# A transformer block's first microseconds: one input tile held back, and its neighbours reordered around the attention weights

## The chip, the cores and the metric

The kernel runs on one core of a Trainium2 chip. The metric is device time in microseconds (us) from start to end of one execution; before the change it is 512.29 us, the median of three runs (512.12 to 512.51). The core has a matrix engine (TensorE, "PE" in the profile, with its weight loads as "PEld"), a vector engine (VectorE, "DVE"), a scalar engine (ScalarE, "ACT"), GpSimd ("POOL") and a synchronising engine (SyncE, "SP") that here mostly starts transfers. Transfers between device memory and on-chip memory run on the core's 16 DMA engines; they are started from a queue of SyncE ("SPq") or of ScalarE ("ACTq").

## The reference

For 2,048 tokens of width 576 the block normalises the input, and adds linear attention with 32 heads and a gated feed-forward part (4,608 wide) to it:

```
xn  = layernorm(x)                                   # 2048 x 576
q, k, v = split(xn @ wqkv)                           # 32 heads of 18
phi = lambda t: where(t > 0, t + 1, exp(t)) + 1e-6
kv  = sum_s phi(k)[s] outer v[s];  z = sum_s phi(k)[s]
o   = (phi(q) @ kv) / (phi(q) . z + 1e-6)
out = x + o @ wo + (gelu(xn @ w_gate) * (xn @ w_up)) @ w_down
```

## The kernel before

**Tiling.** The tokens are handled as 16 tiles of 128 (`NS`), each tile lying on the 128 partitions. One tile of x is 128 rows of 576 bf16, 144 KB. The weights `wqkv` are held as three blocks, Q (0), K (1) and V (2); `load_w` (L107, L108) brings one block in two transfers, 576 KB for rows 0 to 511 and 72 KB for the rest. The V part isn't multiplied tile by tile: a matrix G, the sum over tokens of xn times phi(k), is collected instead (L294), and V's weights come in later.

**Stages.** The first stage goes over the 16 tiles: statistics (L212, two halves, then L215), the reciprocal deviation on ScalarE (`rstd`, L219 and L220), the normalisation (L233 on VectorE; for odd tiles from 3 on, L228 on ScalarE), a transposition to `xnT`, the projections K and Q (L263, ten matmuls of 128x288 each), exp (L270) and phi (L275), and G. Tiles 0 and 1 are transposed by TensorE into PSUM (L248) and copied out (L252), the later ones by DMA. Then G is finished and multiplied with V's weights, and the feed-forward part follows: four chunks of 512 tokens, each with gate and up products (L325) and the down products (L688), in which TensorE reads weights that were loaded some blocks ahead.

**The head.** At the top, SyncE starts tile 0, K's weights, tiles 2 and 3 in one transfer, Q's weights, and tiles 4 to 7, in that order; ScalarE starts tile 1, and then loads the table of its functions (L112). VectorE clears a part of the weights' tile (L118) and fills three constants. TensorE meanwhile multiplies an identity matrix with itself, `NWARM` = 38 times (`spin`, L132), work whose result is never read and which keeps the engine active until the first real work arrives. `spin(2)` comes once more between tile 0's transposes and K's first matmul.

**What sets the order.** From there the order of the instructions on every engine comes from a small planner in the kernel (`in_order`). Each step has an engine, an assumed duration, a rank (its due time in tiles), the steps that it follows, and for those that need a transfer the assumed time of arrival: `X_AT` for tiles of x, `W_AT` for K's and Q's weights. The planner goes through time, and on the engine that is free first takes the step of lowest rank that may start. A tile's `lead` shifts the ranks of its statistics and normalisation. These numbers only set the order; on the chip each instruction waits for what it needs. An engine works its instructions in the order written, so one that waits holds up those behind it.

Of the kernel before, what the change touches and what calls it, by code (L numbers as in the profile page):

```python
# [35 lines left out]
GUB = 2  # L36
NWBUF = 4
WDS = 3
NWARM = 38
TD = 2  # L40
XW = 640
KLO = HP + 1
# [15 lines left out]
def kernel(  # L58
# [11 lines left out]
    nc = tc.nc  # L70
# [19 lines left out]
    x_sb = persist.tile([P, NS, D], BF16, name="x_sb")  # L90

    def load_x(n0, cnt, on=nc.sync):
        on.dma_start(x_sb[:, n0:n0 + cnt, :], x_view[:, n0:n0 + cnt, :])  # L93
# [11 lines left out]
    def load_w(which):  # L105
        c = slice(which * D, (which + 1) * D)
        nc.sync.dma_start(wqkv_sb[:, 0:4, c], A_wqkv[0:512, c].rearrange("(kt p) c -> p kt c", p=P))  # L107
        nc.sync.dma_start(wqkv_sb[0:HP, 4, c], A_wqkv[512:576, c])  # L108

    load_x(0, 1)  # L110
    load_x(1, 1, nc.scalar)
    nc.scalar.preload_act_table_set("natural_log_exp_and_others")  # L112
    load_w(1)
    load_x(2, 2)
    load_w(0)
    load_x(4, 4)

    nc.vector.memset(wqkv_sb[HP:P, 4, :], 0.0)  # L118

    ident = const.tile([P, P], BF16, name="ident")  # L120
    make_identity(nc, ident[:])
# [7 lines left out]
    def spin(count):  # L129

        for _ in range(count):
            nc.tensor.matmul(ps_all[:, 7, 0:P], lhsT=ident[:], rhs=ident[:], start=True, stop=True)  # L132

    spin(NWARM)

# [61 lines left out]
    def z_add(n):  # L197
        nc.gpsimd.tensor_tensor(  # L198
            out=z_bf[:] if n == NS - 1 else z_sum[:], in0=pk[:, 0, 1:D + 1] if n == 1 else z_sum[:], in1=pk[:, n, 1:D + 1],
            op=ALU.add,  # L200
        )
# [7 lines left out]
    def ln_half(n, h):  # L209
        if h == 0:  # L210
            ln_raw[n] = asmall.tile([P, 2, nc.vector.BN_STATS_DIM], F32, name="stats")
        nc.vector.bn_stats(out=ln_raw[n][:, h, :], in_=x_sb[:, n, h * HALF:(h + 1) * HALF])  # L212

    def ln_aggr(n):
        nc.vector.bn_aggr(out=mv[:, n, :], in_=ln_raw[n][:])  # L215

    def ln_rstd(n):
        r = rstd[:, n:n + 1]
        nc.scalar.activation(out=r, in_=mv[:, n, 1:2], func=ACT.Ln, bias=eps_ln[:], scale=1.0)  # L219
        nc.scalar.activation(out=r, in_=r, func=ACT.Exp, scale=-0.5)  # L220

    def ln_bias(n):
        nc.gpsimd.tensor_scalar(
            out=nbias[:, n:n + 1], in0=mv[:, n, 0:1], scalar1=rstd[:, n:n + 1], scalar2=-1.0, op0=ALU.mult, op1=ALU.mult,
        )

    def ln_norm_act(n):
        nc.scalar.activation(  # L228
            out=xn[:, n, 0:D], in_=x_sb[:, n, :], func=ACT.Identity, bias=nbias[:, n:n + 1], scale=rstd[:, n:n + 1],
        )  # L230

    def ln_norm(n, c0=0, c1=D):
        nc.vector.tensor_scalar(  # L233
            out=xn[:, n, c0:c1], in0=x_sb[:, n, c0:c1], scalar1=mv[:, n, 0:1], scalar2=rstd[:, n:n + 1],
            op0=ALU.subtract, op1=ALU.mult,
        )
# [8 lines left out]
    def transposes(n, k0=0, k1=KT, b=None):  # L245
        b = TP_BANK[n] if b is None else b
        for kt in range(k0, k1):
            nc.tensor.transpose(tp_bank(b)[:, kt, :], xn[:, n, kt * P:(kt + 1) * P], ident[:])  # L248

    def tp_copy(n, k0=0, k1=KT, b=None, copy=acopy):  # L250
        b = TP_BANK[n] if b is None else b
        copy(out=xnT[:, k0:k1, n * P:(n + 1) * P], in_=tp_bank(b)[:, k0:k1, :])  # L252

    def dma_transposes(n):
        nc.sync.dma_start_transpose(xnT[:, :, n * P:(n + 1) * P], xn[:, n, 0:640])
# [4 lines left out]
    def kq_mm(n, which, hf):  # L260
        c = which * D + hf * HALF
        for kt in range(KT):
            nc.tensor.matmul(  # L263
                ps_all[:, KQ_BANK[which] + hf, :HALF], lhsT=xnT[:, kt, n * P:(n + 1) * P],
                rhs=wqkv_sb[:, kt, c:c + HALF], start=(kt == 0), stop=(kt == KT - 1),
            )

    def kq_exp(n, which, hf):
        e = e_tiles[n, which, hf] = awork.tile([P, HALF], F32, name="phi_e", tag="phi_e", bufs=8)
        nc.scalar.activation(  # L270
            out=e[:], in_=ps_all[:, KQ_BANK[which] + hf, :HALF], func=ACT.Exp, bias=neg1[:], scale=1.0,
        )

    def kq_phi(n, which, hf):
        nc.vector.scalar_tensor_tensor(  # L275
            out=(pq, pk)[which][:, n, which + hf * HALF:which + (hf + 1) * HALF], in0=e_tiles[n, which, hf][:], scalar=1.0,
            in1=ps_all[:, KQ_BANK[which] + hf, :HALF], op0=ALU.min, op1=ALU.max,
        )
# [12 lines left out]
    def g_accumulate(n, pieces):  # L291
        for kt, ps_ in pieces.items():
            for b, col, d0, w in ps_:
                nc.tensor.matmul(  # L294
                    ps_all[:, b, col:col + w], lhsT=xn[:, n, kt * P:(kt + 1) * P], rhs=pk[:, n, 1 + d0:1 + d0 + w],
                    start=(n == 0 and col == 0), stop=(n == NS - 1), skip_group_check=True,
                )
# [134 lines left out]
    def step(name, *args, **kw):  # L432
        steps[name] = _Step(*args, **kw)

    X_AT = [3.65, 4.20, 6.40, 6.40] + [9.50] * 4
    W_AT = {1: 5.50, 0: 7.60}

    for n0 in range(8, NS, 2):
        step(("x", n0), "SP", 0.50, n0 - 5.5, [], lambda n0=n0: load_x(n0, 2), ready=1.6 * n0 + 2.0, tail=3.0)
    for n in range(NS):  # L440
        lead = {0: -9.0, 1: 0.5, 2: -0.5, 3: -0.5}.get(n, 0.0)
        after_x = [("x", n // 2 * 2)] if n >= 8 else []
        x_at = X_AT[n] if n < 8 else 0.0
        for h in range(2):
            step(("stats", n, h), "DVE", 0.41, n - 2.2 + lead, after_x, lambda n=n, h=h: ln_half(n, h), ready=x_at)
        step(("aggr", n), "DVE", 0.21, n - 2.1 + lead, [("stats", n, 0), ("stats", n, 1)], lambda n=n: ln_aggr(n))
        step(("rstd", n), "ACT", 0.49, n - 2.1 + lead, [("aggr", n)], lambda n=n: ln_rstd(n))
        if n < TD:
            for i, (k0, k1, eng) in enumerate([(0, 3, "ACT"), (3, KT, "ACT" if n else "DVE")]):
                b = TP_BANK[n] - i  # L450
                step(("norm", n, i), "DVE", 0.25, n - 2.1 + lead, [("rstd", n)],
                     lambda n=n, k0=k0, k1=k1: ln_norm(n, k0 * P, min(k1 * P, D)))
                step(("tp", n, i), "PE", 0.20, n - 1.5 + lead, [("norm", n, i)],
                     lambda n=n, k0=k0, k1=k1, b=b: transposes(n, k0, k1, b))
                step(("xnT", n, i), eng, 0.30 if i else 0.48, n - 0.88 + lead, [("tp", n, i)],
                     lambda n=n, k0=k0, k1=k1, b=b, eng=eng: tp_copy(n, k0, k1, b, acopy if eng == "ACT" else vcopy))
            ready = [("xnT", n, 0), ("xnT", n, 1)]
        else:
            if n % 2:
                step(("bias", n), "POOL", 0.15, n - 2.1, [("rstd", n)], lambda n=n: ln_bias(n))  # L460
                step(("norm", n), "ACT", 0.65, n - 2.1, [("bias", n)], lambda n=n: ln_norm_act(n))
            else:
                step(("norm", n), "DVE", 0.43, n - 2.1, [("rstd", n)], lambda n=n: ln_norm(n))
            step(("xnT", n), "SP", 2.10, n - 1.9, [("norm", n)], lambda n=n: dma_transposes(n), tail=1.7)
            ready = [("xnT", n)]
        for which, rank in ((1, n), (0, n + 0.6)):
            for h in range(2):
                r = rank + h / 100
                free = [("phi", n - 1, which, h)] if n else []
                step(("mm", n, which, h), "PE", 0.615, r, ready + free, lambda n=n, w=which, h=h: kq_mm(n, w, h),  # L470
                     ready=W_AT[which], tail=0.15)
                step(("exp", n, which, h), "ACT", 0.49, r + 0.10, [("mm", n, which, h)],
                     lambda n=n, w=which, h=h: kq_exp(n, w, h))
                step(("phi", n, which, h), "DVE", 0.44, r + 0.15, [("exp", n, which, h)],
                     lambda n=n, w=which, h=h: kq_phi(n, w, h))
        if n > 0:
            idle = [("norm", n + 4) if n % 2 == 0 else ("bias", n + 4)] if n + 4 < NS else []
            step(("z", n), "POOL", 1.40, n + 2.0, [("phi", m, 1, h) for m in (0, n) for h in range(2)] + idle,
                 lambda n=n: z_add(n))
        step(("G", n), "PE", 0.75, n + 1.15, [("phi", n, 1, 0), ("phi", n, 1, 1)], lambda n=n: g_accumulate(n, G_A))  # L480
    step(("spin",), "PE", 0.11, -1.0, [("tp", 0, 1)], lambda: spin(2))

    def in_order(steps):

# [281 lines left out]
```

## Time and profile before

| what | us |
|---|---|
| time, median of 3 runs | 512.29 |
| span of the profiled run | 510.7 |
| TensorE busy | 505.2 |
| VectorE busy | 211.4 |
| ScalarE busy | 136.9 |
| tile 0 of x, issue to landing | 3.0 |
| tile 1 of x, issue to landing | 2.9 |
| first statistics start | 3.86 |
| K's first matmul starts | 6.91 |
| Q's first matmul starts | 8.80 |

Times within a run count from the span's start. Busy time of an engine is the time in which one of its instructions is in progress. An arrow in a list of waits names what ended a wait; "idle before" is the idle time of the engine ahead of an instruction. The granted clock of TensorE is 1.000 of full speed over the run.

### The profile page before, as it was taken

The numbers are of one execution on the slowest core, as the hardware profiler recorded it, in microseconds if no ns is written. First come the engines' busy times: TensorE is split into PE (matmuls) and PEld (weight loads), VectorE is DVE, ScalarE is ACT, GpSimd is POOL, SyncE is SP. The second block draws the span as 40 slices with busy tenths as digits, with TensorE's granted clock in tenths as the row PEclk, the third lists the DMA queues.
The fourth block names the chain that finished last, engine by engine and source line by source line (L and its number), as shares of the span: only waits on it lengthen the run. The fifth ranks groups of instructions, "written<-read, shape, count | busy, mean of one in ns | idle before, by whom it ended". The sixth has DMA issues, their size and how long they took to land.

```text
span 510.7 us, 10656 instructions
## 1 busy us (share of the span) xinstructions
PE 505.2 (99%) x4489; PEld 304.6 (60%) x4489; DVE 211.4 (41%) x447; ACT 136.9 (27%) x267; POOL 25.5 (5%) x40
## 2 busy tenths in 40 slices
PE   7999999999999999999999999999999999999997
PEld 6888854444587744444677644444777444445774
DVE  7887455555400045565200254555100356544101
ACT  5887533332310022332100023323000133232000
POOL 3344200000000000000000000000000000000000
PEclk9999999999999999999999999999999999999999
DMA  6633839999500057666300256566100565540000
GB/s 210 144 67 55 244 97 273 279 276 272 147 13 12 1 170 172 154 167 165 87 12 13 69 168 173 156 174 154 35 12 1 144 166 159 164 130 14 13 12 24
DMA packets 119002, 61.26 MB, mean 120 GB/s; under 512 B 25698, under 2 KB 118122, under 8 KB 118954
## 3 DMA queue, kind: packets, MB, share of 16 engines
q1 hardware_dynamic: 118810, 60.43, 45.0%
q8 instruction: 35, 0.57, 0.5%
q10 hardware_dynamic: 144, 0.15, 0.2%
q14 instruction: 13, 0.11, 0.1%
HBM read 52.86 MB, written 2.36 MB: 108 GB/s over the span
## 4 chain that ended last, share of the span: by engine, by line
PE 98%; DMA 1%; SPq 0%; issue 0%; DVE 0%
PE ps_all L325 55%; PE ps_all L688 28%; PE ps_all L263 7%; PE ps_all L294 3%; PE ps_all L693 3%; DMA wqkv_sb<-in_A_wqkv_dram 1%; PE ps_all L676 0%; PE ps_all L301 0%; PE ps_all L374 0%; PE ps_all L628 0%; SPq L93 0%; SPq L108 0%; SPq L107 0%; DVE res L702 0%; PE ps_all L362 0%
## 5 line engine op out<-in xcount | busy, mean ns | idle before, releaser
L325 PE MATMUL ps_all<-xnT,wg 64*128 64x512 bf16 x1152 | 272.1, 376 | 0.0
L325 PE MATMUL ps_all<-xnT,wu 64*128 64x512 bf16 x1152 | 271.6, 376 | 0.0
L617 ACT ACTIVATE gl<-ps_all 128x512 f32<-128x512 f32 x144 | 86.0, 597 | 308.9 <-PE ps_all L325 308.8
L618 DVE TENSOR_TENSOR hT<-ps_all,gl 128x512 bf16<-128x512 f32 x144 | 99.6, 692 | 130.9 <-ACT gl L617 130.4
L325 PEld LDWEIGHTS <-wu 64*128 64x128 bf16 x1152 | 108.4, 94 | 68.1
L325 PEld LDWEIGHTS <-wg 64*128 64x128 bf16 x1152 | 108.4, 94 | 67.7
L688 PE MATMUL ps_all<-wd_sb,hT 128*128 128x288 bf16 (+2 forms) x1152 | 147.1, 286 | 0.0
L688 PEld LDWEIGHTS <-hT 128*128 128x128 bf16 x1152 | 110.8, 98 | 30.9 <-issue 1.2
L702 DVE TENSOR_TENSOR res<-ps_all,x_sb 128x288 bf16<-128x288 f32 (+2 forms) x32 | 13.8, 455 | 146.3 <-PE ps_all L693 88.1
L325 PE MATMUL ps_all<-xnT,wr 64*128 64x512 bf16 x288 | 54.7, 376 | 0.0
L263 PE MATMUL ps_all<-wqkv_sb,xnT 128*128 128x288 bf16 x320 | 42.1, 286 | 0.6 <-DMA wqkv_sb<-in_A_wqkv_dram 0.3
L263 PEld LDWEIGHTS <-xnT 128*128 128x128 bf16 x320 | 30.5, 98 | 7.9 <-ACT xnT L252 0.5
L270 ACT ACTIVATE phi_e<-ps_all,neg 128x288 f32<-128x288 f32 x64 | 30.9, 495 | 9.1 <-PE ps_all L263 6.3
L325 PEld LDWEIGHTS <-wr 64*128 64x128 bf16 x288 | 14.0, 94 | 16.7
L693 PE MATMUL ps_all<-m_sb,pqT 128*128 128x288 bf16 (+2 forms) x128 | 20.9, 286 | 0.0
L294 PE MATMUL ps_all<-hT,xn 128*128 128x288 bf16 (+4 forms) x144 | 18.8, 274 | 0.0
L275 DVE SCALAR_TENSOR_TENSOR pq<-phi_e,ps_all 128x288 bf16<-128x288 f32 x32 | 14.2, 450 | 7.7 <-ACT phi_e L270 7.4
L198 POOL TENSOR_TENSOR z_sum<-z_sum,hT 128x576 f32<-128x576 f32 x13 | 16.2, 1244 | 4.7 <-DVE hT L275 4.4
L294 PEld LDWEIGHTS <-xn 128*128 128x128 bf16 x144 | 14.0, 98 | 3.6 <-issue 0.2
L275 DVE SCALAR_TENSOR_TENSOR hT<-phi_e,ps_all 128x288 bf16<-128x288 f32 x32 | 14.1, 454 | 2.4 <-ACT phi_e L270 2.3
L693 PEld LDWEIGHTS <-pqT 128*128 128x128 bf16 x128 | 12.4, 98 | 3.3
L212 DVE BATCH_NORM_STATS2 stats<-x_sb 128x6 f32<-128x288 bf16 x32 | 13.6, 440 | 1.9 <-DMA x_sb<-in_A_x_dram 1.9
(66 smaller groups left out, 125.3 us busy)
## 6 DMA issues: line engine op xcount, KB each, us to landing
wg<-in_B_w_gate_dram SPq DMA_DIRECT2D x72, 256.0 KB, 3.0
wu<-in_B_w_up_dram SPq DMA_DIRECT2D x72, 256.0 KB, 3.6
wd_sb<-in_B_w_down_dram SPq DMA_DIRECT2D x12, 432.0 KB, 5.4
wr<-in_B_w_gate_dram SPq DMA_DIRECT2D x72, 32.0 KB, 2.8
wr<-in_B_w_up_dram SPq DMA_DIRECT2D x72, 32.0 KB, 3.1
out_dram<-res SPq DMA_DIRECT2D x15, 144.0 KB, 1.8
wqkv_sb<-in_A_wqkv_dram SPq DMA_DIRECT2D x3, 576.0 KB, 4.6
x_sb<-in_A_x_dram SPq DMA_DIRECT2D x5, 288.0 KB, 3.1
```

Source lines behind the costliest of these rows:

```text
L198: nc.gpsimd.tensor_tensor(out=z_bf[:] if n == NS - 1 else z_sum[:], in0=pk[:, 0, 1:D + 1] if n == 1 else z_sum[:], in1=pk[:, n, 1:D + 1], ...
L212: nc.vector.bn_stats(out=ln_raw[n][:, h, :], in_=x_sb[:, n, h * HALF:(h + 1) * HALF])
L263: nc.tensor.matmul(ps_all[:, KQ_BANK[which] + hf, :HALF], lhsT=xnT[:, kt, n * P:(n + 1) * P], rhs=wqkv_sb[:, kt, c:c + HALF], start=(kt == ...
L270: nc.scalar.activation(out=e[:], in_=ps_all[:, KQ_BANK[which] + hf, :HALF], func=ACT.Exp, bias=neg1[:], scale=1.0,)
L275: nc.vector.scalar_tensor_tensor(out=(pq, pk)[which][:, n, which + hf * HALF:which + (hf + 1) * HALF], in0=e_tiles[n, which, hf][:], scala ...
L294: nc.tensor.matmul(ps_all[:, b, col:col + w], lhsT=xn[:, n, kt * P:(kt + 1) * P], rhs=pk[:, n, 1 + d0:1 + d0 + w], start=(n == 0 and col = ...
L325: return nc.tensor.matmul(self.outs[i], lhsT=self.lhs(i, rows, kt), rhs=self.rhs(i, rows, kt), start=start, stop=stop, skip_group_check=True,)
L617: nc.scalar.activation(out=gl[:], in_=ps_all[:, b[0], :], func=ACT.Gelu_apprx_tanh)
L618: nc.vector.tensor_tensor(out=hT[:, GUB * k + i, :], in0=ps_all[:, b[1], :], in1=gl[:], op=ALU.mult)
L688: nc.tensor.matmul(self.acc(hf), lhsT=hT[:, f, j * P:(j + 1) * P], rhs=wd_sb[:, f, self.parts[hf]], start=(f == 0 and not paired), stop=Fa ...
L693: nc.tensor.matmul(self.acc(hf), lhsT=pqT[:, c, self.ts], rhs=m_sb[:, c, self.parts[hf]], start=False, stop=(paired and c == 3), skip_grou ...
L702: nc.vector.tensor_tensor(out=self.res[:, hs], in0=self.acc(hf), in1=x_sb[:, self.n, hs], op=ALU.add)
```

## The change

The change rearranges the transfers at the top and tells the planner. Tile 1's load moves behind a write of one column of its own destination by VectorE (`memset(x_sb[:, 1, 0:1])`); as both write the same place, the load has to wait for it, and with this it starts after tile 0's load instead of together with it. Tiles 2 and 3 are loaded one by one: tile 2 ahead of Q's weights, tile 3 behind them. The planner gets other times of arrival: tile 0 at 3.05 instead of 3.65, tile 2 sooner, tile 3 and tiles 4 to 7 later, Q's weights later. The number of spins before the first transposes falls from 38 to 32, and that of the spins after them rises from 2 to 5. The purpose is to have the first tile there sooner, to have Q's weights not stand behind a tile that isn't needed yet, and to order the head's instructions by what arrives when.

```diff
-NWARM = 38
+NWARM = 32
...
     load_x(0, 1)
-    load_x(1, 1, nc.scalar)
     nc.scalar.preload_act_table_set("natural_log_exp_and_others")
     load_w(1)
-    load_x(2, 2)
+    load_x(2, 1)
     load_w(0)
+    load_x(3, 1)
     load_x(4, 4)
 
     nc.vector.memset(wqkv_sb[HP:P, 4, :], 0.0)
+    nc.vector.memset(x_sb[:, 1, 0:1], 0.0)
+    load_x(1, 1, nc.scalar)
...
-    X_AT = [3.65, 4.20, 6.40, 6.40] + [9.50] * 4
-    W_AT = {1: 5.50, 0: 7.60}
+    LEAD = (-9.0, 0.5, -0.5, -0.5)
+    X_AT = [3.05, 4.30, 6.00, 8.60] + [10.40] * 4
+    W_AT = {1: 5.60, 0: 8.10}
...
-        lead = {0: -9.0, 1: 0.5, 2: -0.5, 3: -0.5}.get(n, 0.0)
+        lead = LEAD[n] if n < 4 else 0.0
...
-    step(("spin",), "PE", 0.11, -1.0, [("tp", 0, 1)], lambda: spin(2))
+    step(("spin",), "PE", 0.30, -1.0, [("tp", 0, 1)], lambda: spin(5))
```

In the instruction lists of the two kernels VectorE has one instruction more, TensorE three matmuls less, and the rest is the same in number but for the one transfer that became two. On TensorE all five transposes of tile 1 now stand ahead of Q's matmuls of tile 0, where two of them stood between Q's halves; on VectorE the first half of tile 1's statistics stands ahead of tile 0's normalisation and the second behind it, where both stood ahead; and further on one block of G has moved ahead of one half of a projection.

## The prediction

> **What bounds the kernel now.** I read the page first for who is busy, then the granted clock, then the stretches of the span, then who TensorE waits for, then the chain of the first 16 us, then its instructions in order of time.
>
> Busy time and the chain that ended last, from the page: TensorE is busy 505.2 of 510.7 us, and 98% of the chain is TensorE.
>
> ```profile
> PE 505.2 (99%) x4489; PEld 304.6 (60%) x4489; DVE 211.4 (41%) x447; ACT 136.9 (27%) x267; POOL 25.5 (5%) x40
> PE 98%; DMA 1%; SPq 0%; issue 0%; DVE 0%
> ```
>
> The stretches (length, then busy time of PE, PEld, DVE, ACT, POOL, then granted clock, DMA share, GB/s). The reader is to see that from 8.80 us on TensorE has no idle time until 507.5: 3.20 of 3.20, 48.00 of 48.00, 440.00 of 440.00. All that can be removed ahead of the tail lies before 8.80 us.
>
> ```profile
> 5.45:6.00 0.55, 0.00 (x0) 0.00 (x1) 0.55 (x3) 0.04 (x1) 0.38 (x2) 1.00 1.04 394
> 6.91:8.80 1.89, 1.57 (x13) 1.14 (x14) 1.81 (x7) 1.38 (x6) 0.00 (x0) 1.00 1.06 381
> 8.80:12.00 3.20, 3.20 (x28) 2.59 (x28) 3.07 (x10) 2.85 (x9) 0.26 (x1) 1.00 0.37 97
> 12.00:60.00 48.00, 48.00 (x407) 38.94 (x405) 37.31 (x101) 38.28 (x91) 19.93 (x21) 1.00 0.53 121
> 60.00:500.00 440.00, 440.00 (x3933) 252.68 (x3932) 164.66 (x317) 92.07 (x160) 0.57 (x1) 1.00 0.45 120
> ```
>
> The waits of TensorE over the whole run (total us, times, longest): four, all in the head.
>
> ```profile
> PE ps_all L132 <- POOL ident masks.py:199: 1.4, 1, 1.4
> PE ps_all L248 <- DVE xn L233: 0.6, 1, 0.6
> PE ps_all L263 <- DMA wqkv_sb<-in_A_wqkv_dram: 0.3, 1, 0.3
> PE ps_all L263 <- ACT xnT L252: 0.3, 1, 0.3
> ```
>
> The chain of the first 16 us (start, length, what). From it the reader learns which head wait ends last: not the first tile's normalisation but Q's weights. They are issued at 2.97, land 5.79 us later at 8.76, and Q's first matmul starts at 8.80; after it the chain is matmuls alone.
>
> ```profile
> 2.97 5.79 DMA wqkv_sb<-in_A_wqkv_dram
> 8.76 0.04 issue
> 8.80 0.77 PE ps_all L263 x5
> 9.57 0.11 PE ps_all L248 x2
> 9.68 1.84 PE ps_all L263 x15
> ```
>
> The same stretch in order of time (start, busy us, engine, what, idle before). K's ten matmuls of tile 0 start at 6.91, three us after the first tile's statistics (3.86), and end before 8.80.
>
> ```profile
> 3.86 0.82 DVE L212 BATCH_NORM_STATS2 stats<-x_sb 128x6 f32<-128x288 bf16 x2 [1.90 <-DMA x_sb<-in_A_x_dram]
> 5.53 0.65 DVE L233 TENSOR_SCALAR xn<-x_sb,mv,rstd 128x384 bf16<-128x384 bf16 x2
> 6.91 1.40 PE L263 MATMUL ps_all<-wqkv_sb,xnT 128*128 128x288 bf16 x10 [0.28 <-ACT xnT L252]
> ```
>
> **What the Trainium skill says.** First, "DMA: Bandwidth & Descriptors", section "Issuing engines are not separate DMA queues": transfers begun by different engines run on the same 16 DMA engines and interleave. The trace agrees: between 2.6 and 3.4 us the scalar queue (tile 1) and the sync queue (tile 0) both move packets, and the total is 347 GB/s, near the 370 GB/s that one queue reaches from 3.4 to 8.8 us. So tile 1 takes bandwidth from tile 0. Second, "TensorE: Matmul & The Clock Gate", Part 1: the array runs at half rate until about 3.4 us of activity have passed, with the change near 4 us and some 500 ns of play. Here the spins take 314 ns in the record until 4.6 us and 219 from about 5.0: warm some 3.5 us after the first one at 1.42. Third, the same page, "Architectural detail", says that VectorE and ScalarE work strictly in order; their timelines agree, and it matters for where tile 1's statistics stand.
>
> **The change part by part.**
>
> *Tile 1 behind a memset.* It adds one memset of 128x1 on VectorE (the like ones take 0.06 us) after the 0.78 us memset that ends at 1.82. Tile 1's load can so be issued at about 2.0 instead of 0.79; the table load on ScalarE, 1.28 us long, may stand ahead of it and end near 2.1. Nothing is queued behind it on ScalarE before the first rstd at 4.96. From issue to landing such a load took 2.9 us, hence 4.9; the first half of its statistics now stands ahead of tile 0's normalisation on VectorE, so a landing later than about 4.5 would hold that up. I take 4.5 to 4.9.
>
> *Tile 0 alone.* Its 144 KB no longer share with another 144 KB. At 370 GB/s that is 147,456 B / 370 = 0.40 us; but the first packets are slow (108 GB/s from 1.8 to 2.6 us), so I bound the gain from 0.3 to 0.7 and take 0.5: statistics at 3.35. The chain to K (6.91 - 3.86 = 3.05 us) then starts K at 6.40. If tile 1 lands at 4.9, the half statistics (0.41) delay this by up to 0.4, to 6.8. K's weights landed at 1.25 + 4.6 = 5.85, and the bytes ahead of them stay the same, so they are no wait.
>
> *Tile 3 behind Q's weights.* The bytes ahead of Q's weights fall by one tile, 0.40 us at 370 GB/s. Tile 1's bytes stay ahead of them, since it is issued before they are. So 8.76 becomes 8.36. The slower ramp, with one queue where there were two, may give back some 0.05 to 0.1: 8.41, and Q can start at 8.45.
>
> *Is anything later than this?* K starts at 6.40 and takes ten times about 0.1225 (twenty take 2.45 in the chain), to 7.63. Tile 1's transposes need its normalisation, which follows tile 2's statistics on VectorE. Those began at 6.76 before, with two tiles in one transfer; with one tile ahead it lands 0.4 sooner, so they start at 6.4. From them to the end of tile 1's normalisation took 8.31 - 6.76 = 1.55, so 7.95, and all five transposes are done by 8.15. That is 0.3 before Q can start: the weights still end last.
>
> *Order of the head.* The planner's new arrivals put all five transposes of tile 1 ahead of Q; before, two (0.11 us) stood between Q's halves. They move into the wait for the weights: 0.11 us. Further down one block of G moves ahead of one projection half; same instructions, no cost as long as VectorE (37.3 of 48 us busy) and ScalarE (38.3) keep up, as they do now.
>
> *Spins.* Six fewer at about 0.106 us each before the first transposes, three more (0.06 each when warm) after them. They run in TensorE's idle time, so I cost them at nothing; 32 cold spins end near 1.42 + 3.4 = 4.83, right where the clock changed (4.6 to 5.0). If it changes a window later, K and the transposes run at half rate.
>
> *Tile 3 late.* It lands where the pair's end and Q's weights landed together, about 9.0. Its statistics began at 9.06 before, so no wait is added. Its DMA transpose is wanted after 16 us.
>
> **Sum.** Q 8.80 - 8.45 = 0.35, plus the 0.11 of moved transposes: 0.46 us. TensorE has no idle time behind it, so this passes to the end: 512.29 - 0.46 = **511.8**.
>
> **The rivals.**
>
> 1. *A new wait takes the place (no gain).* Tile 1 is late, VectorE stands before its statistics, and Q waits for K and the transposes. With landing at 5.3, normalisation at 5.75, K at 7.1 to 8.35, tile 1's transposes at 8.7, Q at 8.8: 512.2 to 512.3. For it: the strict order on VectorE. Against it: 0.4 us of slack, since K may slip from 6.40 to 6.8 unseen.
> 2. *Cold clock (slower).* With the clock up only one 3.4 us window later, at about 8.3, K costs 1.0 more; Q starts at about 9.0, 0.1 later than the old sequence allowed: 512.4. If it misses that window too, the work from 9.0 to 11.7 runs at half rate, 1.35 more: 513.7. For it: the spins end just where the clock changed. Against it: the window was nearly full by then, and three times within 0.4 us of each other show no such jumps.
> 3. *More than the bytes say.* Both queues' slow start was contention; everything lands 0.3 sooner still: gain 0.8, 511.5. A gain over 1.02 us needs Q at 7.9, which the bytes ahead of it at 370 GB/s don't allow.
>
> **How the numbers follow.** Forecast (gain 0.2 to 0.7) 0.68; rival 1, 0.12; rival 2, 0.10, half of it past 513.3; rival 3, 0.10. The range takes the forecast, rival 3 and the near end of rival 1: 511.4 to 512.4. A bound of 0.2% is 1.02 us: faster by more 0.05 (arrivals that I misjudge in several places), slower by more 0.05 (the cold clock), the rest within.
>
> **What would show it.** In the changed profile: first statistics near 3.35; K's first matmul at 6.3 to 6.8; the wait before Q's first matmul put down to the weights, ending near 8.45; ten and more matmuls back to back after it with no transposes between; no TensorE idle from there to the end. Wrong if TensorE waits on VectorE or ScalarE between 9 and 60 us (the reordered middle), if spins of 314 ns are still seen after 5.5 us, or if Q's weights land at 8.7 in spite of fewer bytes ahead.

## The result, and the profile after

The changed kernel takes **514.54 us** (median of four runs, 514.42 to 515.42) against 512.2 for the kernel before (512.01 to 512.51 in four runs beside them): ratio 1.0049, 95% interval 1.0031 to 1.0066. It is 2.3 us slower; 511.8 was forecast, with 512.4 as the upper end of the range.

Where the time went is best asked of the waits of TensorE first. Over the whole run of the changed kernel (engine and line, releaser: total us, times, longest) there are two:

```profile
PE ps_all L250 <- DVE xn L235: 1.8, 1, 1.8
PE ps_all L134 <- POOL ident masks.py:199: 1.4, 1, 1.4
```

The wait for Q's weights is gone, as intended, and so is the one for ScalarE. In their place the wait for VectorE's first normalisation has grown from 0.6 to 1.8 us. The stretches of the changed kernel (columns as for the kernel before):

```profile
6.91:8.80 1.89, 1.89 (x15) 1.44 (x14) 1.66 (x8) 0.98 (x3) 0.00 (x0) 1.00 1.10 397
8.80:12.00 3.20, 3.20 (x22) 2.44 (x21) 2.34 (x8) 2.41 (x7) 0.00 (x0) 1.00 0.16 63
12.00:60.00 48.00, 48.00 (x407) 38.96 (x406) 38.61 (x104) 38.20 (x94) 19.45 (x22) 1.00 0.54 115
60.00:500.00 440.00, 440.00 (x3938) 253.04 (x3937) 165.22 (x319) 93.84 (x162) 1.28 (x2) 1.00 0.46 120
```

TensorE is again fully busy from 8.80 on, so the loss lies ahead of 12 us. But 8.80 to 12.00 holds 22 matmuls where it held 28, in the same 3.20 busy us: they take longer on average. "Busy" doesn't tell an engine at full clock from one at half, and the column of the granted clock shows 1.00 in both; only the duration of one instruction does.

The chain of the first 16 us of the changed kernel (start, length, what; the "issue" gaps left out):

```profile
0.79 1.18 ACT L111
1.98 3.98 DMA x_sb<-in_A_x_dram
...
5.98 0.04 DVE stats L214
...
6.35 0.38 DVE xn L235
...
8.02 2.41 PE ps_all L265 x10
10.43 0.53 PE ps_all L250 x5
10.96 2.46 PE ps_all L265 x20
```

The reader is to see two things. Tile 1's load (1.98 + 3.98 = 5.96) now ends last in the head, not Q's weights; it releases half a statistics instruction of tile 1 that stands on VectorE ahead of tile 0's normalisation (6.35). And K's ten matmuls take 2.41 us, the twenty after them 2.46: K runs at half speed ("cold" below; "warm" is full speed). The same stretch in order of time shows both; tile 0's own statistics were done by 3.9:

```profile
3.08 0.82 DVE L214 BATCH_NORM_STATS2 stats<-x_sb 128x6 f32<-128x288 bf16 x2 [1.11 <-DMA x_sb<-in_A_x_dram]
5.98 0.46 DVE L214 BATCH_NORM_STATS2 stats<-x_sb 128x6 f32<-128x288 bf16 x1 [1.83 <-DMA x_sb<-in_A_x_dram]
6.35 0.60 DVE L235 TENSOR_SCALAR xn<-x_sb,mv,rstd 128x384 bf16<-128x384 bf16 x2
7.85 2.58 PE L265 MATMUL ps_all<-wqkv_sb,xnT 128*128 128x288 bf16 x10
```

**A landmark.** G of tile 0 (L294 before, L296 after) starts at 11.36 in the kernel before and at 13.26 after. From there everything is the same: first feed-forward matmul 55.50 us later in both, the last group of matmuls 440.53 after that in both. So the profiled runs differ by these 1.90 us alone, and every kernel below can be judged by its start of G:

| kernel | G of tile 0, us | profiled run, us | difference |
|---|---|---|---|
| before | 11.36 | 512.53 | 501.17 |
| before, second profile (12) | 11.16 | 512.29 | 501.13 |
| after | 13.26 | 514.42 | 501.16 |

By this rule the median of before, 512.2, belongs to a start of G near 11.05. The profile shown in the prediction is of a run 0.3 us above that median.

### The profile page after: what moved, and what is told of

It is laid out like the page before. It is cut to its first block, busy times and chain, and to the rows that moved or that the text cites. A ratio compares the mean times of both kernels' runs of the same rounds, so it can differ in the third digit from the quotient of the medians.

```text
span 512.7 us, 10653 instructions
## 1 busy us (share of the span) xinstructions
PE 506.5 (99%) x4486; PEld 305.3 (60%) x4486; DVE 211.9 (41%) x448; ACT 137.2 (27%) x267; POOL 25.5 (5%) x40
## 4 chain that ended last, share of the span: by engine, by line
PE 98%; DMA 1%; ACT 0%; DVE 0%; issue 0%
PE ps_all L327 55%; PE ps_all L691 28%; PE ps_all L265 8%; PE ps_all L296 3%; PE ps_all L696 3%; DMA x_sb<-in_A_x_dram 1%; PE ps_all L679 0%; PE ps_all L303 0%; PE ps_all L376 0%; PE ps_all L250 0%; ACT L111 0%; PE ps_all L631 0%; PE ps_all L134 0%; DVE xn L235 0%; DVE res L705 0%
## 5 line engine op out<-in xcount | busy, mean ns | idle before, releaser
L265 PE MATMUL ps_all<-wqkv_sb,xnT 128*128 128x288 bf16 x320 | 43.2, 291 | 0.0
L296 PE MATMUL ps_all<-hT,xn 128*128 128x288 bf16 (+4 forms) x144 | 18.8, 274 | 0.0
L296 PEld LDWEIGHTS <-xn 128*128 128x128 bf16 x144 | 14.0, 98 | 3.6 <-issue 0.2
L696 PEld LDWEIGHTS <-pqT 128*128 128x128 bf16 x128 | 12.4, 98 | 3.3
```

Source lines behind the costliest of these rows:

```text
L265: nc.tensor.matmul(ps_all[:, KQ_BANK[which] + hf, :HALF], lhsT=xnT[:, kt, n * P:(n + 1) * P], rhs=wqkv_sb[:, kt, c:c + HALF], start=(kt == ...
L296: nc.tensor.matmul(ps_all[:, b, col:col + w], lhsT=xn[:, n, kt * P:(kt + 1) * P], rhs=pk[:, n, 1 + d0:1 + d0 + w], start=(n == 0 and col = ...
L696: nc.tensor.matmul(self.acc(hf), lhsT=pqT[:, c, self.ts], rhs=m_sb[:, c, self.parts[hf]], start=False, stop=(paired and c == 3), skip_grou ...
```

## The experiments

The theory after reading this: two independent losses, each of which the prediction had named as a rival, add up. "The hold" is the one-column write with tile 1's load behind it. **A**, the clock: with 32 spins TensorE's clock rises too late and K runs at half speed. **B**, the order: tile 1 arrives later than 4.9, and its half statistics stand ahead of tile 0's normalisation. Rivals: one of them alone explains it (the other being hidden behind it), or the load's late landing has another cause than its position.

All results in one table (median and spread of the runs; ratio to the kernel before with its 95% interval, which need not be the quotient of the two medians; start of G and of K in the profiled run; "rest" is that run's time less its start of G).

| kernel | median, us (runs) | ratio | K | G | rest |
|---|---|---|---|---|---|
| after | 514.54 (514.42 to 515.42; 4) | 1.0049 [1.0031, 1.0066] | 7.85 | 13.26 | 501.16 |
| 1 after, 38 spins | 514.36 (513.49 to 514.90; 15) | 1.0037 [1.0029, 1.0045] | 8.09 | 12.19 | 501.73 |
| 2 after, tile 1's statistics behind | 513.03 (512.41 to 513.99; 12) | 1.0006 [0.9994, 1.0018] | 6.24 | 11.23 | 501.18 |
| 3 both | 513.18 (512.35 to 514.26; 12) | 1.0016 [1.0006, 1.0026] | 6.09 | 11.19 | 501.16 |
| 4 after, no hold, 32 spins | 512.84 (512.17 to 513.92; 12) | 1.0007 [0.9995, 1.0019] | 7.08 | 12.30 | 501.16 |
| 5 no hold, 38 spins | 512.79 (512.61 to 513.23; 12) | 1.0009 [1.0000, 1.0018] | 6.92 | 11.02 | 501.67 |
| 6 hold first on VectorE, 38 spins | 512.91 (512.66 to 513.38; 20) | 1.0009 [1.0002, 1.0016] | 6.93 | 11.02 | 501.68 |
| 7 tile 1 on SyncE's queue, 38 spins | 513.42 (512.88 to 514.32; 10) | 1.0017 [1.0007, 1.0027] | 6.55 | 12.43 | 501.15 |
| 8 before, 32 spins | 513.60 (512.02 to 513.77; 9) | 1.0019 [1.0010, 1.0029] | 7.15 | 12.18 | 501.12 |
| 9 as 5, no second spins | 512.37 (512.17 to 514.06; 12) | 0.9998 [0.9986, 1.0010] | 6.91 | 11.00 | 501.17 |
| 10 as 5, two second spins | 512.28 (512.15 to 514.04; 12) | 1.0001 [0.9991, 1.0010] | 6.91 | 11.00 | 501.15 |
| 11 before, tiles 2 and 3 split | 512.08 (512.03 to 513.94; 12) | 0.9999 [0.9990, 1.0007] | 6.92 | 10.88 | 501.15 |
| 13 as 6, two second spins | 512.20 (512.17 to 514.00; 14) | 0.9999 [0.9990, 1.0008] | 6.93 | 11.02 | 501.16 |
| 14 as 13, GpSimd's writes late | 511.92 (511.66 to 512.23; 21) | 0.9993 [0.9986, 0.9999] | 6.56 | 10.80 | 501.20 |
| 15 as 11, GpSimd's writes late | 512.12 (511.87 to 512.35; 13) | 0.9996 [0.9988, 1.0004] | 6.63 | 11.04 | 501.16 |
| 16 before, GpSimd's writes late | 512.03 (511.84 to 512.54; 13) | 0.9994 [0.9986, 1.0002] | 6.68 | 10.79 | 501.16 |

### The clock and the order, each undone (1 to 5, and 8)

1, 38 spins again in the changed kernel:

```diff
-NWARM = 32
+NWARM = 38
```

> The changed kernel with 38 spins in place of 32, all else the same. Theory A (two losses that add: tile 1's late landing blocks VectorE ahead of tile 0's normalisation, and TensorE's clock stays at half rate over the first 10 K matmuls because the spins end too soon): the clock rises by 5 us as before, the late tile stays; about 1.2 us come back, 513.3. Rival B (the clock alone is the loss): 512.0 to 512.2. Rival C (the late tile alone, the cold clock hidden behind it): 514.5, no change.

In the traced run K's ten matmuls are back at 1.40 us, and G starts 1.07 sooner than in the changed kernel (12.19 for 13.26). Tile 1 still lands late (1.98 + 4.4), and the wait stays: `DVE xn L235` 1.5 us. A new loss of 0.57 came in behind G (see "rest", 501.73; taken up under 9 and 10), which leaves a gain of 0.50 in this run, 513.92. The median, 514.36, is only 0.18 below that of the changed kernel, where 1.2 had been expected: twelve of the 15 runs lie 0.4 to 1.0 us above the traced one, and what they lose is not shown.

2, the half statistics of tile 1 moved by hand behind tile 0's normalisation and copy, 32 spins:

```diff
+    for h in range(2):
+        order.remove(("stats", 1, h))
+        order.insert(order.index(("xnT", 0, 1)) + 1 + h, ("stats", 1, h))
```

> The changed kernel with both halves of tile 1's statistics moved behind tile 0's normalisation and copy on VectorE, 32 spins as changed. Theory A: tile 0's transposes come at about 5.1 instead of 6.8 and K at about 6.2; if the clock then rises soon after 5, 512.1; if it stays low over K, about 512.8. Rival B (clock alone): the gap after the spins shrinks from 1.8 to 0.3 us, so 512.1 as well, but only if K's matmuls are seen at full rate. Rival C: 512.1 with K's matmuls still at half rate.

> Statistics moved as in the run before and 38 spins. Theory A: both losses gone; tile 1 still lands at about 6.0, so its transposes end near 8.7 and Q starts there, against 8.80 with two transposes still to come before: 512.1, at most 0.2 below the kernel before. Rivals B and C: the same as the better of the two single mends.

In the traced runs both (3 has 38 spins too) start K ahead of the prediction's 6.40, at 6.24 and 6.09, without tile 1 arriving any sooner: it is the place in VectorE's order that made the late tile costly. They gain no more, since tile 1's own transposes then wait for it (in 3: two waits for VectorE, 1.0 us together; Q at 8.74). But each of these traces is of the run with the least time of 12. The medians lie 0.6 and 0.8 us above them, and 3, for which 512.1 was expected, is 1.0 above the kernel before beside it: the new place alone doesn't make the held tile harmless in a typical run. That the spread, 512.35 to 514.26 in 3, follows tile 1's landing is likely but not traced.

4 and 5, the hold taken out (ScalarE starts tile 1 at the top, as before), with 32 and 38 spins; everything else as in the change:

```diff
     load_x(0, 1)
+    load_x(1, 1, nc.scalar)
...
-    nc.vector.memset(x_sb[:, 1, 0:1], 0.0)
-    load_x(1, 1, nc.scalar)
```

> The changed kernel with tile 1's load issued by ScalarE at the top as in the kernel before, no one-column write; transfers 2 and 3 split, planner's times and 32 spins as changed. Theory A: tile 1 lands at about 3.7 and no longer blocks; tile 0 lands at 3.8 as before, its transposes come at about 6.0, 1.1 us after the spins end. If that leaves the clock low: K lasts to 9.6 and the time is about 513.5. If the clock is up: Q waits for its weights to about 8.4 and the time is 511.8. Rival C (late tile alone): 511.8 whatever the clock does.

> As the run without the hold, with 38 spins in place of 32. That run fell into two groups, 512.2 and 513.5 to 513.9. Theory A (the second group is a half-rate clock over K, because 32 spins end at 4.8): with 38 spins the upper group nearly vanishes and the median is 512.2 or below. Rival (the groups come from the transfers or from the planner's new order): they stay, about half and half. What the split of tiles 2 and 3 brings by itself then shows too: 0.35 to 0.5 below the kernel before by the prediction's arithmetic, so 511.8; 512.2 if Q's weights don't come sooner.

4 splits into two groups, six runs of 512.17 to 512.21 and six of 513.46 to 513.92; the profiled run is of the upper one. In it K takes 2.58 us; that K is warm in the lower six is inferred from their times. 5 has one group, and K takes 1.40 in its trace. Its median, 512.79, misses the 512.2 that was expected; the half microsecond is the subject of 9 and 10. The four starts of G make a square:

| | 32 spins, K cold | 38 spins, K warm | clock |
|---|---|---|---|
| held (after, 1) | 13.26 | 12.19 | 1.07 |
| not held (4, 5) | 12.30 | 11.02 | 1.28 |
| late tile | 0.96 | 1.17 | |

In these traces, one for each corner, both losses are real, of about the same size, and nearly additive: 13.26 - 11.02 = 2.24. Against the profiled run of before the sum is 1.90, as 5 starts G 0.34 sooner than that run had it (11.36 - 11.02). The medians are less even: at 38 spins the late tile costs 1.57 (514.36 for 512.79), and in the held kernel the spins 0.18 (514.54 for 514.36), with what the other runs of 1 lose unexplained.

The two are not independent either. In 2, with 32 spins, TensorE idles 0.2 us between spins and transposes; only the first three of K's ten matmuls are slow (422, 447 and 441 ns), and G starts at 11.23, against 11.19 in 3 with 38 spins. In the three traces in which all ten are slow, TensorE idles longer there: 1.8 us in the changed kernel, 1.0 in 4, 1.1 in 8. So the wait that a late tile makes may itself have helped to keep the clock low, or the clock rose sooner in that run of 2 by chance: behind 38 spins 1.5 us of idle time left K warm (1), and no run changes the idle time alone.

8 asks for A in the other kernel: before, with 32 spins and nothing else.

```diff
-NWARM = 38
+NWARM = 32
```

> The kernel before with 32 spins in place of 38 and nothing else changed. Theory A (the clock's rise needs activity up to about 5 us, whose phase varies from run to run): two groups, one at 512.1, and one some 1.2 to 1.5 above it that holds a third or more of the runs, where the kernel before has one run in ten near 514. Rival (spins are not needed that long, the clock loss comes from the long wait of TensorE behind the late tile only): 512.1 throughout.

Eight of nine runs take 513.30 to 513.77, one 512.02. K's matmuls of the profiled run (duration of one in ns, minimum, median, maximum; first and last start), ahead of them those of the kernel before:

```profile
L263 PE MATMUL ps_all<-wqkv_sb,xnT x10: 286/286/297, 6.9 to 8.0; 128*128 128x288 bf16 x10
```

```profile
L263 PE MATMUL ps_all<-wqkv_sb,xnT x8: 423/447/448, 7.1 to 8.8; 128*128 128x288 bf16 x8
```

The same instruction in the same place takes half as long again in the record, and the ten take 2.46 us from the first to the last instead of 1.40. Six spins of 0.1 us each, on an engine that has nothing else to do, are worth some 1.4 us (513.60 for 512.2 in the medians); the change had taken them out.

### Why tile 1 lands so late (6 and 7)

6 puts the hold's write first on VectorE (ahead of the 0.78 us memset), with 38 spins:

```diff
+    nc.vector.memset(x_sb[:, 1, 0:1], 0.0)
+    load_x(1, 1, nc.scalar)
     nc.vector.memset(wqkv_sb[HP:P, 4, :], 0.0)
-    nc.vector.memset(x_sb[:, 1, 0:1], 0.0)
-    load_x(1, 1, nc.scalar)
```

> The changed kernel with the one-column write as VectorE's first instruction, ahead of the 0.78 us memset, and 38 spins. Tile 1's load can then be issued at about 1.2, ahead of K's weights (1.25), not at 1.98 behind both of their transfers. Theory A (a load is served after the bytes that were issued before it, whichever queue it came from): tile 1 lands at about 4.0 to 4.3, the statistics no longer block, 512.0. Rival (a load from ScalarE's queue is served late whenever SyncE's queue holds work): it lands at about 5.9 again, 514.4 as with 38 spins and the late hold.

The load is issued at 1.0 instead of 1.98 and takes 2.7 us instead of 4.0. The queues show how (packets, MB, share of the 16 engines; q1 is SyncE's queue, q10 ScalarE's). Here from 2.6 to 3.4 us:

```profile
q1 hardware_dynamic: 133, 0.14, 54.4%
q10 hardware_dynamic: 140, 0.14, 50.5%
```

In the changed kernel, from 2.6 to 3.4 us SyncE's queue is alone, and ScalarE's moves nothing until 4.8; these are 2.6 to 3.4, 4.8 to 5.2 and 5.2 to 5.6:

```profile
q1 hardware_dynamic: 78, 0.08, 71.0%
...
q10 hardware_dynamic: 95, 0.11, 75.7%
q1 hardware_dynamic: 63, 0.05, 36.4%
...
q1 hardware_dynamic: 97, 0.11, 77.2%
q10 hardware_dynamic: 49, 0.04, 28.5%
```

In the changed kernel a load that is issued behind the 576 KB of K's weights (1.25) has its bytes moved behind them, though its queue is another one and empty: its first packet comes at 4.9, and at 4.5 to 4.7 in 1, 2 and 3. In 6, issued ahead of them, its first comes at 2.5, and the two queues share. The prediction leaned on the Trainium skill, "DMA: Bandwidth & Descriptors", section "Issuing engines are not separate DMA queues", for transfers of two engines interleaving. The traces agree only for loads issued close together, as in 6; for the held one the order of issue decided. The median of 6, 512.91 where 512.0 was expected, doesn't show the sooner landing yet, for the reason found under 9 and 10.

7 asks whether the second queue is needed: tile 1 from SyncE, right behind tile 0.

```diff
     load_x(0, 1)
+    load_x(1, 1)
...
-    nc.vector.memset(x_sb[:, 1, 0:1], 0.0)
-    load_x(1, 1, nc.scalar)
```

> The changed kernel with tile 1 loaded from SyncE's queue right behind tile 0 and ahead of K's weights, no one-column write, 38 spins. Theory A: tile 0 lands at 3.1 as with the hold and tile 1 at about 3.7; no block on VectorE; K at about 6.2, Q when its weights land, one more issue (0.4 us) behind than now, near 8.5 to 8.8: 511.8 to 512.2. Rival (one queue alone feeds the transfers too thinly at the start, so that all comes later): tile 0 early, but K's weights after 6.2 and Q's at 9 or later: 512.5.

First statistics at 3.05, K at 6.55; but then the chain has

```profile
3.43 6.51 DMA wqkv_sb<-in_A_wqkv_dram
```

Q's weights land at 9.94, and G starts at 12.43. From 2.6 to 3.4 us 225 GB/s were moved, from 3.4 to 6.0 us 300, and from 6 to 8.8 us 320, against 364, 380 and 370 in experiment 5. With everything on one queue the same bytes moved more slowly in this trace. The changed kernel too moved little while ScalarE's queue was held back (102 GB/s from 2.6 to 3.4 us, 347 in the kernel before). But a single queue isn't slow as such: SyncE's alone moved 378 GB/s from 3.4 to 4.8 us in the changed kernel. What slowed the transfers in 7 and at the start is not shown.

### Half a microsecond behind G (9 and 10)

Experiments 1, 5 and 6 lose another 0.51 to 0.57 us behind the start of G. In 5 a new wait stands there:

```profile
PE ps_all L264 <- DMA xnT<-xn: 0.3, 1, 0.3
```

and the chain has `9.24 4.21 DMA xnT<-xn`: tile 2's transpose by DMA takes 4.2 us, where it takes 2.7 in the kernel before. While it runs, 11.2 to 11.6 us, the queues of 5 are

```profile
q1 hardware_dynamic: 133, 0.03, 34.5%
q8 instruction: 1, 0.02, 15.2%
```

one 16 KB packet of instructions among its packets. The theory: a fetch of TensorE's instructions falls among them, and its place depends on how many instructions stand before, that is, on the spins: 43 in 1, 5 and 6, 40 in the kernel before. 9 and 10 take only second spins away, none and two for the five:

```diff
-    step(("spin",), "PE", 0.30, -1.0, [("tp", 0, 1)], lambda: spin(5))
+    step(("spin",), "PE", 0.30, -1.0, [("tp", 0, 1)], lambda: spin(2))
```

> The run without the hold and with 38 spins, now without the five spins between tile 0's transposes and K. Theory D (found in the two runs before: one instruction fetch for TensorE, a single packet of about 1 us on one DMA engine, falls among the packets of tile 2's DMA transpose, which then lands 4.2 us after issue in place of 2.6, and TensorE waits 0.3 us for it): ten TensorE instructions fewer put the fetch some 0.6 us later, behind the transpose; it lands after 2.6, no wait, 0.5 us less: 512.2 where the run with five spins had 512.7. Rival (the late landing comes from the order of the loads of x): 512.7 again, with 4.2 us.

> The same with two spins there, as many as the kernel before has, so the fetch falls some 0.36 us later than with five. Theory D: it falls at the very end of the transpose's packets, at about 11.6 to 11.8, so the time is 512.2 or, in a part of the runs, 512.7. Rival: 512.7 throughout.

In both the wait is gone, the transpose takes 2.7 us, and the rest is 501.15 to 501.17; the packet comes after 11.6, behind the transpose's. That fewer instructions remove the loss is shown; that the packet itself delays the transpose rests on where it lies in the traces, and nothing here moved the packet alone. All traces fit, though: in the five with 43 spins (1, 3, 5, 6, 7) the packet falls among the transpose's, which takes 3.15 to 4.25 us to land; in the thirteen others it comes behind their last, and the transpose takes 2.7. In 3 and 7 it lands at 13.1 and 12.4, in time, and no loss shows in the rest (501.16, 501.15).

10 also closes the account of the change. It has the split loads and the new order, but neither the hold nor the changed spins, and takes 512.28 against 512.31 of the kernel before beside it: as far as the interval, 0.9991 to 1.0010, can tell, the hold and the spins are the whole loss.

### What the split and the order give (11 and 12)

```diff
-    load_x(2, 2)
+    load_x(2, 1)
     load_w(0)
+    load_x(3, 1)
```

> The kernel before with tiles 2 and 3 loaded one by one, tile 3 behind Q's weights, and nothing else changed. If the split brings Q's weights 0.40 us sooner, as the prediction has it, Q's first matmul starts at about 8.4 and the time is 0.3 to 0.4 below the kernel before: 511.8. If the weights come no sooner, or tile 3's statistics, which this order has ahead of a phi of tile 0, now hold VectorE up: 512.1 to 512.3.

> The kernel before, unchanged, for a second profile of it. The one on record belongs to a time of 512.5, and most of its runs are at 512.0 to 512.3. If this one is such a run, it shows where the 0.3 to 0.5 us between them lie: theory, in the arrival of Q's weights or in tile 2's transpose; rival, in the tail.

With the split alone Q starts at 8.32 without a wait for weights, and G at 10.88; in the second profile of the kernel before the weights land at 8.56 (8.76 in the first), and G starts at 11.16. In the runs the difference is not resolved: 512.08 against 512.31 beside it, ratio 0.9999 [0.9990, 1.0007]. The wait that the change was to remove is 0.3 us long in the first profile of the kernel before (a run of 512.53), and about 0.1 in the second (512.29).

### Why K starts at 6.91 in so many kernels (13 to 16)

One step of the prediction stayed unexplained: "tile 0 alone ... starts K at 6.40". In seven kernels with tile 1 in time and the clock up K starts at 6.91 to 6.93, whether its first statistics start at 3.4 (6, 13) or at 3.7 to 3.9 (11, before). The timeline of 13 (6 with two second spins) shows what pins it:

```profile
4.85 0.33 POOL L187 TENSOR_SCALAR_AFFINE_SELECT bmask<-bmask 128x126 f32<-128x126 f32 x1
5.06 1.13 DVE L235 TENSOR_SCALAR xn<-x_sb,mv,rstd 128x384 bf16<-128x384 bf16 x2 [0.28 <-ACT rstd L222]
5.13 0.58 POOL L192 MEMSET g_sb<- 128x576 bf16 x1
5.64 0.21 POOL L195 MEMSET ones<- 128x128 bf16 x1
```

Tile 0's normalisation starts at 5.06, but its first half alone takes 0.90 us and ends at 5.96, just after GpSimd's row of writes ends at 5.85. In the kernel before it starts at 5.53 and its first half ends at 5.95: the same end. The Trainium skill, "SBUF — State Buffer", section "SBUF: two separate sides", says that VectorE, in some of its modes, and GpSimd share a pair of ports under an exclusive lock: the instruction that starts first keeps it to its end, and the other waits. The trace agrees in that the half is held up, 0.90 us for its usual 0.37 to 0.38. It doesn't show which of the writes holds it: waiting for the last one's end, 5.85, and then taking 0.37 would give 6.22, not 5.96. To test whether the writes are the cause, GpSimd's writes of the mask, of a constant row group of `g_sb` and of the ones, all read only behind the first stage, move to just ahead of its first sum:

```diff
-    nc.gpsimd.memset(bmask[:], 1.0)
...
-    nc.gpsimd.memset(g_sb[:, 4, :], 0.0)
-    nc.gpsimd.memset(ones[:], 1.0)
...
+        if n == 1:
+            late_consts()
```

> The hold at the head of VectorE's order, 38 first spins and 2 second spins, GpSimd's writes where they were (the control of the next run). Theory of the held-up normalisation: tile 0 lands near 3.4, its normalisation starts near 5.0 and still ends at 5.95, K starts at 6.9; with the second spins cut tile 2's transpose is back at 2.6 to 2.7 us, so 512.1 to 512.3. Rival, that the end at 5.95 follows the arrival of a tile: normalisation ends with tile 0, near 5.4, K near 6.4, 511.8.

> As the run before, with GpSimd's writes of the head's mask, of the constant row group of g_sb and of the ones moved behind the zeroing that K's output needs. Theory of the held-up normalisation: its first half takes 0.34 to 0.42 us instead of 0.93, ends near 5.4, K starts near 6.4, Q by 8.3 to 8.4, G of tile 0 at 10.7: 511.7 to 511.9. Rival, that another thing pins K (or the arrival of Q's weights takes over at 8.4 to 8.6): 512.1 to 512.3.

In 14 the same instruction reads

```profile
4.99 0.62 DVE L239 TENSOR_SCALAR xn<-x_sb,mv,rstd 128x384 bf16<-128x384 bf16 x2 [0.28 <-ACT rstd L226]
```

0.62 us for the two halves instead of 1.13, done by 5.61. So the writes were what held it. K starts at 6.56, 0.37 sooner than in 13, and G at 10.80, 0.22 sooner. It isn't 6.40, since TensorE is still cold there: it goes from the spins straight into the transposes, whose starts lie 0.42 us apart from first to last instead of 0.30, and K's first matmuls are cold too (ten take 1.68 us). Medians: 512.20 to **511.92**. This is the one version that beats both kernels beyond its interval, by 0.07% of the kernel before, and barely (0.9993 [0.9986, 0.9999]).

> The kernel before with tiles 2 and 3 split around Q's weights as in the change and GpSimd's writes moved, nothing held. Theory: normalisation of tile 0 ends some 0.25 us sooner (near 5.7), K near 6.66, Q near 8.3, G of tile 0 at 10.6 to 10.8: 511.8 to 512.0. Rival, that Q's weights or tile 1 bind: 512.1 as with the split alone.

> The kernel before with GpSimd's writes moved only. Theory: K near 6.66, but Q waits for its weights, which land near 8.56 to 8.8, so the wait grows by what K gains: 512.0 to 512.3. Rival, that an earlier K is worth its full 0.25 us: 511.9 to 512.05.

In both, the two halves take 0.62 us. In 15 normalisation and K follow as expected (K at 6.63, 0.29 sooner than in 11), but in the profiled run Q waits for its weights until 8.48 and G starts at 11.04: the gain is given to another wait, and the median, 512.12, is about that of 11. In 16 K starts at 6.68. In 11, where tile 0 was there at the same time (first statistics at 3.68, here 3.67), the writes held K to 6.92; in the first profile of the kernel before, with 3.86, they hardly held it (0.65 us for the two halves). What moving them is worth so depends on when tile 0 comes. The weights came before Q needed them (Q at 8.23), and G starts at 10.79; the median, 512.03, lies in the ranges of both theories. Their intervals hold 1. What binds at 8.2 to 8.8 us, weights or normalisation, seems to change from run to run: the two traces of the kernel before alone have the weights at 8.76 and 8.56.

## Why the prediction was wrong, by its own steps

**Tile 1 behind a memset: failed.** "I take 4.5 to 4.9" for its landing; it was 5.96. The issue time was right (2.0 forecast, 1.98 measured). The error was the 2.9 us from issue to landing, taken over from a load that was issued ahead of K's weights, for one that is issued behind them: 4.0 us. The prediction had the condition right, that a landing later than 4.5 would hold up VectorE, and then didn't carry it beyond 5.3. In rival 1 it gives K at 7.1, with Q at the old 8.8; the same sum with 5.96 gives K at about 7.8, which is what was measured (7.85), and Q behind it, later than before. Its size in G: 0.96 to 1.17 us.

**Spins: failed.** "I cost them at nothing" because they lie in idle time. Their worth isn't time but the state in which they leave the clock. The prediction saw that 32 spins end where the clock had changed, and gave that case 0.10; in the kernel before, 32 spins cost the clock in eight of nine runs. "Three times within 0.4 us of each other show no such jumps" was the wrong evidence: those were runs with 38 spins, which say nothing on the margin at 32. Nor do equal times show a steady clock: in the traces with 38 spins the first fast matmul comes between 4.2 us (3) and 7.0 (7 and 14). The sign it named, spins of 314 ns after 5.5 us, is there: the second spins, from 7.28 on, take 314 ns each, and K's matmuls 447. Its size in G, 1.07 to 1.28 us, is near the 1.0 that rival 2 had K cost more (measured: 2.41 for 1.40). Rival 2's near end let only 0.1 of that through to the end, as the wait for the weights was to hide the rest; in the changed kernel K ends at 10.4, and no such wait is left.

**Rivals kept apart: failed.** Each was priced alone, as the other part being as forecast (512.3 and at worst 513.7). They share nothing that would make them exclude each other, and they came together.

**Tile 0 alone: right in part.** Statistics at 3.08 (3.35 forecast), from a load of 2.3 us. That "starts K at 6.40" fails for a reason the prediction lacked: GpSimd's writes hold the normalisation until 5.95 in any case, unless it starts ahead of the last of them (2 and 3, at 4.73 in 2) or they move (14). In the changed kernel itself the late tile hid this, as the normalisation started only at 6.35.

**Tile 3 behind Q's weights: right, and small.** 0.35 us sooner was forecast; without the late tile Q starts at 8.56 (5) and 8.32 (11) for 8.80 and 8.60. The profile of before caught a late arrival, though: in the second the weights land 0.2 sooner, so there is less to gain, and the split alone is not resolved from no change.

**Moved transposes: no gain seen.** 0.11 us were forecast because they would lie in the wait for the weights. With that wait gone there is nothing to hide them in: from K's first matmul to G it is 4.10 us in 5 with the new order and 3.96 in 11 with the old.

**No idle from 8.8 on, and the passing of a head's gain or loss to the end: right.** The difference between time and start of G is 501.12 to 501.20 in every kernel without the late transpose.

## What to carry to other kernels

Price a held-back load by what was issued ahead of it by then, on the other queue too, not by the duration it had when issued first; and ask of any wait that is put ahead of the critical instruction, on an engine that works in order, what happens if it is a microsecond longer. Cutting the work that keeps a clock up by a sixth cost nothing in some runs here and 1.2 us or more in others (4 and 8), so it is tested by itself, and looked for in the duration of one instruction, as neither busy time nor the granted clock showed it. When an end stays at the same time whatever its start, look for what the other engines do up to that time.

## What the runs showed of the hardware that was not expected

- In the traces with 38 spins K is warm from its first matmul, but for 7 and 14, where the first two or three are cold. With 32, all ten are cold in three traces (after, 4, 8) and three in one (2); by their times, K was warm in one of nine runs of 8 and six of twelve of 4. The changed kernel's K ran at 447 ns a matmul with the granted clock shown as 1.00.
- Alone, SyncE's queue moved 102 (after) and 225 GB/s (7) from 2.6 to 3.4 us, but 378 from 3.4 to 4.8 (after); two queues moved 347 (before) and 364 (5) from 2.6 to 3.4.
- The first half of a normalisation, 0.38 us otherwise, took 0.90 while GpSimd wrote constants, and ended 0.11 us after the last of them.
- A transpose by DMA took 3.15 to 4.25 us instead of 2.7 in the five traces in which a packet of instructions fell among its own.
